# Keys and queries of the second token parity: seven block products in one stage instead of eight in two

## The chip, the core and the metric

The kernel runs on one core of one Trainium2 chip. The metric is the time of one execution on the device in microseconds; the program before has a median of 607.33 us in three runs.

## What is computed

A gated mix of two branches over one sequence of 2048 tokens with 512 channels, all in float32:

```python
g = sigmoid((x * gate_w).sum(-1, keepdims=True))
# A: attention, 32 heads of 16 channels; token s sees the 8 tokens s, s-2, ..., s-14
q, k, v = split(x @ wqkv)                  # 512 -> 3 x 512
logits = einsum(q[s], k[s - 2*w]) * 16**-0.5          # w = 0..7, masked below 0
a = (softmax(logits) @ v) @ wo
# B: gated feed-forward, 1792 hidden channels
b = (gelu(x @ w_gate) * (x @ w_up)) @ w_down
out = g * a + (1 - g) * b
```

## The kernel before

**Order of the work.** Because the window steps by two tokens, even and odd tokens (the two "parities", `par` 0 and 1, 1024 tokens each) never meet, and the kernel does one after the other: `project`/`values` (keys, queries, values, gate), then `ffn(par)` with 14 slices `f` of 128 hidden channels each. Every float32 operand of a product on TensorE is split into a high and a low part ("hi", "lo", both fp32r), and each product is three matmuls: hi x hi, lo x hi, hi x lo. A split is a copy on ScalarE (ACT) for the high part and a subtraction on VectorE (DVE) for the low part; in two places (`operands`, `down_w`) the low part is made with the negated copy on ACT and then a DMA on POOL's queue that adds the raw operand to it.

**Seven products for eight.** The value projection (`values`) and gate/up (`gate_up`) use the Strassen-Winograd scheme: the operands are cut into 2 x 2 blocks, four sums of token blocks (`s1` to `s4`, made by `sums_x`) and four of weight blocks (`t1` to `t4`) are formed, and seven block products take the place of eight. In the second parity the keys and queries are done in the plain way, in two halves of the heads: `project(1)` does the first half, 8 blocks of tokens with `qkv_mm` (4 channel chunks x 3 matmuls each), between the feed-forward part of the first parity and the values; `project_one(1, jj)` does the second half, 8 blocks again, as "pieces" inside the slices f = 0 and 1 of `ffn(1)`. The end of `ffn(0)` up to the beginning of the values of the second parity is called the turn here: the steps `before()`, `again()` and `split_kq()` load and split the tokens and weights of the second parity there.

**Attention.** It is done on DVE alone, head by head group, in 8 units: (0,0) to (0,3) for the first parity, (1,0) to (1,3) for the second. A unit has scores (`scores`, 4 pairs of a product L398 and a reduction L401), a softmax and a weighted sum (`mix`, L436 to L449), and leaves through a scratch tensor `OS` in memory; `channels` reads it back as the operand of the output projection. The generator `attention()` hands its steps out as the matmuls are emitted: every piece of TensorE work ends in `pull(budget)`, and steps are handed out until the budget is used up (a score product counts 2.3). The budgets are written out by hand: `PACE` scales those of `gate_up` and `down`. What is handed out gets a lower priority by `BEHIND` = 150 places, and a scheduler that simulates the program puts the instructions of each engine in their final order. `paced(ins)` tells that scheduler not to put an instruction ahead of the last matmul emitted; it is no wait on the chip.

**The end.** `out_first` does the output projection of the first parity, `down(1, 6, ...)` the last part of the feed-forward product, and `finish` adds the output projection of the second parity, 4 units x 8 token blocks x 3 matmuls (`by_unit`, L868). The last unit's part (1,3) is the last that `finish` needs.

**Buffers that matter here.** 8 banks of PSUM: four named `p`, and `acc0` to `acc3`. `A`, `S`, `d`, `g0`, `g1`, `hh`, `hl`, `c`, `rt` are rings of tiles in SBUF that all stages share.

Of the kernel before, what the change touches and what calls it, by code (L numbers as in the profile page):

```python
# [16 lines left out]
P = 128  # L17
# [12 lines left out]
NU = D // UC  # L30
WARM = 31
BEHIND = 150
PACE = (0.9, 1.12)
LOAD = 4.0
BT = 4
MASKED = -1e9 * DH ** 0.5
# [8 lines left out]
def tile_gated_mix(ctx: ExitStack, tc: tile.TileContext, xt, wqkv, wff, wo, out):  # L45
# [124 lines left out]

    VW, VR, VO, SLOT = 2 * WQ, {}, {}, []

    def room_v():

        for tag, n in ("g0", 3), ("g1", 3), *[("c", 1)] * 4:
# [54 lines left out]
    def fetch_v(n):  # L230
        for i in range(2):
            nc.sync.dma_start(VO[n][i].bitcast(F32), VS_W[n][i])


    z = pool.tile([P, 2, NP], F32, name="z")
# [48 lines left out]
    def values(par, bg, step):  # L284
# [26 lines left out]
        for k, (a, b) in enumerate((("a11", "b11"), ("a12", "b21"), ("s1", "t1"), ("s4", "b22"), ("s2", "t2"),  # L311
                                    ("s3", "t3"), ("a22", "t4"))):
            for t in range(BT):
                if k == 0:
                    C[t] = bank(f"acc{t}")
                elif k == 2:
                    Z_[t] = bank("p")
                ps = Z_[t] if 0 < k < 4 else C[t]
                mm(ps, t, a, b, k in (0, 2))
                if k == 0:  # L320
                    Z_[t] = bank("p")
                    copy(Z_[t][:, :WQ], ps[:, :WQ])
                elif k == 2:
                    PS[t] = stage()
                    copy(PS[t][:, :CU], ps[:, :CU])
                elif k == 3:
                    copy(PS[t][:, CU:], ps[:, :CU])
                elif k == 4:
                    US[t] = stage()
                    copy(US[t][:, CU:], ps[:, :CU])  # L330
                elif k == 5:
                    copy(US[t][:, :CU], ps[:, :CU])
                    nc.vector.tensor_tensor(PS[t], PS[t], US[t], op=OP.add)
                    store(PS[t][:, CU:], t, 1)
                    store(PS[t][:, :CU], BT + t, 1)
                else:
                    if k == 1:
                        ST[t] = stage()
                    jj, st = (t, ST[t][:, :CU]) if k == 1 else (BT + t, ST[t][:, CU:])
                    copy(st, ps[:, :CU])  # L340
                    copy(z[:, par, jj:jj + 1], ps[:, CU:WQ - 1])
                    store(st, jj, 0)
                next(bg, None)
                pull((0.77, 0.63)[par])
            step(k)
        for _ in bg:
            pass
# [3 lines left out]
        nc.vector.tensor_scalar_add(en, en, 1.0)  # L351
        nc.vector.reciprocal(g[:, par], en)
        nc.vector.tensor_scalar(gc[:, par], g[:, par], -1.0, 1.0, op0=OP.mult, op1=OP.add)

    def project_one(par, jj):

# [279 lines left out]
    def down(par, gr, t, b):  # L636
# [20 lines left out]
        elif b:  # L657
            if gr == 0:
                RT[BT + t] = tl("rt")
            nc.scalar.activation(RT[BT + t], pp, AF.Copy)  # L660
        pull(1.2 * PACE[par])

    def gate_up(par, f, pieces, do):

# [48 lines left out]
            hidden((f, 1), ge, c22)  # L713
        late.append(last)

    SPLIT = []

    def again(blk, kc):

        split_x(1, blk, kc, copy=lambda *x: paced(nc.vector.tensor_copy(*x)))  # L720
# [1 line left out]
    def early():  # L722

        t = tl("g0")
        for kc in range(3):
            raw = t[:, kc * 512:(kc + 1) * 512]
            load_kq_weights(raw, kc)
            SPLIT.append((kc, raw))

    def split_kq():  # L730
        kc, raw = SPLIT.pop(0)
        hi, lo = WC[0, kc] = next(room)
        split(nc.vector, hi, lo, raw, held)

    def before():

        room_x(1)
        yield
        again(0, 0)
        yield  # L740
        again(0, 2)
        yield
        split_kq()
        SPLIT.append((3, tl("r")))
        load_kq_weights(SPLIT[-1][1], 3)
        yield
        split_kq()

    def ffn(par):
        XOP.update(((n, kc), X[par, blk, kc + k]) for n, blk, k in (("a11", 0, 0), ("a12", 0, 2), ("a22", 1, 2))  # L750
# [2 lines left out]
        for f in range(FC):  # L753
# [2 lines left out]
            def at(i, x, *args):  # L756
                do.setdefault(i, []).append(lambda: x(*args))

            if f > 1:
# [46 lines left out]
        if par:  # L806
            out_first()
            oT = {}
        for b in range(2):
# [138 lines left out]
    room_v()  # L948
    for _ in sums_x():
        pass  # L950
    made = make_v()
# [32 lines left out]
        store_v()  # L984

    values(0, first(), step)
    room = rooms()
    keep(0)
    ffn(0)
    room_v()  # L990
    for n in "b11", "b21", "t1", "b22", "t2":
        fetch_v(n)
# [53 lines left out]
```

## Time and profile before

| | |
|---|---|
| median of 3 runs (lowest, highest) | 607.33 us (606.11, 609.34) |
| the profiled execution: time, span of its instructions | 604.47 us, 602.7 us |
| TensorE (PE) busy, matmuls | 595.9 us, 2791 |
| VectorE (DVE) busy | 530.4 us |
| ScalarE (ACT) busy | 403.1 us |
| POOL busy | 69.0 us |
| mean granted TensorE clock | 0.999 |
| data moved, mean rate | 132.80 MB, 220 GB/s |

Times in the trace count from the first instruction of the profiled execution. `PEld` is the load of TensorE's stationary operand, which overlaps the matmuls. `x30` behind a row is a count of instructions that were merged into it. The span ends at 602.7 us; the execution's own time is 1.77 us more.

### The profile page before, as it was taken

What the parts mean: (1) busy time and instruction counts of PE and PEld (TensorE: products, weight loads), DVE (VectorE), ACT (ScalarE), POOL (GpSimd) and SP (SyncE); (2) the same over time, 40 slices, a digit from 0 to 9 for tenths busy, and PEclk for the clock granted to TensorE, in tenths of its full rate; (3) what the DMA queues carried; (4) which work ended last, traced back from release to release, by engine and by line L of the source; (5) the groups of instructions that cost most, each with busy time, mean ns of one, the idle gap of its engine ahead of it and who ended that gap; (6) DMA issues with size and microseconds to landing.
All of it is one profiled execution on the core that took longest, in us unless ns stands there. A gap on an engine that the chain in (4) does not pass through costs nothing.

```text
span 602.7 us, 8195 instructions
## 1 busy us (share of the span) xinstructions
PE 595.9 (99%) x2791; PEld 498.3 (83%) x2791; DVE 530.4 (88%) x624; ACT 403.1 (67%) x699; POOL 69.0 (11%) x94
## 2 busy tenths in 40 slices
PE   8999999999999999999999999999999999999997
PEld 6898878888888888888898888888888888888885
DVE  6959899997999979999798989997999799989821
ACT  6665666679777797765574467577666876796531
POOL 0150001111111111102000001111111111101300
PEclk9999999999999999999999999999999999999999
DMA  8695987969686886987599979879596869647813
GB/s 293 237 272 185 310 286 219 248 179 269 182 243 193 242 220 191 264 277 254 179 267 316 305 240 262 213 187 271 149 232 189 260 145 257 167 124 173 139 38 140
DMA packets 85592, 132.80 MB, mean 220 GB/s; under 512 B 8111, under 2 KB 50223, under 8 KB 85550
## 3 DMA queue, kind: packets, MB, share of 16 engines
q1 hardware_dynamic: 66190, 100.88, 50.9%
q0 software_dynamic: 10368, 26.81, 23.6%
q10 hardware_dynamic: 8992, 4.59, 2.6%
q8 instruction: 22, 0.36, 0.2%
q14 instruction: 20, 0.16, 0.1%
HBM read 69.83 MB, written 40.46 MB: 183 GB/s over the span
## 4 chain that ended last, share of the span: by engine, by line
PE 78%; DMA 7%; issue 4%; DVE 4%; ACT 3%; SPq 1%; POOL 1%; ACTq 0%; POOLq 0%
PE p L605 37%; PE acc L647 10%; PE p L647 10%; PE acc L247 9%; PE p L868 5%; PE acc L298 2%; DMA r<-wff 2%; PE acc L868 2%; PE p L247 2%; PE p L298 1%; DVE prod L436 1%; DMA out<-s 1%; DMA raw<-ws 1%; DMA g<-vwt 1%; DMA raw<-xt 1%
## 5 line engine op out<-in xcount | busy, mean ns | idle before, releaser
L605 PE MATMUL p<-S,g 128*128 128x512 f32 x672 | 167.6, 389 | 0.3 <-ACT s L610 0.3
L605 PEld LDWEIGHTS p<-S,g 128*128 128x128 f32 x672 | 125.9, 188 | 26.7 <-ACT s L610 0.7
L605 PE MATMUL p<-A,g 128*128 128x512 f32 x504 | 124.8, 389 | 0.0
L605 PEld LDWEIGHTS p<-A,g 128*128 128x128 f32 x504 | 94.5, 188 | 19.5
L398 DVE TENSOR_TENSOR prod<-kq 128x2048 f32<-128x2048 f32 x32 | 72.9, 2277 | 2.8 <-DMA kq<-kq 2.5
L436 DVE TENSOR_TENSOR prod<-v,lg 128x2048 f32<-128x2048 f32 x32 | 72.9, 2277 | 0.5
L401 DVE TENSOR_REDUCE lg<-prod 128x128 f32<-128x2048 f32 x32 | 73.0, 2281 | 0.2
L647 PE MATMUL p<-d,hh 128*128 128x512 f32 x224 | 69.1, 390 | 0.0
L647 PE MATMUL acc<-d,hh 128*128 128x512 f32 x224 | 59.4, 389 | 0.0
L616 ACT ACTIVATE c<-p 128x512 f32<-128x512 f32 x56 | 33.5, 598 | 38.4 <-PE p L605 38.4
L563 POOL DMA_DIRECT2D g<-raw x28 | 24.2, 863 | 259.1 <-ACT g L560 153.6
L647 PEld LDWEIGHTS p<-d,hh 128*128 128x128 f32 x224 | 42.0, 188 | 9.0 <-ACT p L641 0.3
L647 PEld LDWEIGHTS acc<-d,hh 128*128 128x128 f32 x224 | 42.0, 188 | 8.7
L647 PE MATMUL p<-d,hl 128*128 128x512 f32 x112 | 42.1, 389 | 0.0
L624 DVE TENSOR_TENSOR hl<-c,hh 128x512 fp32r<-128x512 f32 x56 | 38.1, 682 | 3.7 <-ACT hh L623 3.4
L623 ACT ACTIVATE hh<-c 128x512 fp32r<-128x512 f32 x56 | 35.0, 626 | 9.0 <-DVE c L621 7.5
L621 DVE TENSOR_TENSOR c<-c 128x512 f32<-128x512 f32 x56 | 38.2, 683 | 3.1 <-ACT c L712 1.7
L610 ACT ACTIVATE s<-p 128x512 f32<-128x512 f32 x56 | 32.9, 595 | 11.9 <-PE p L605 10.7
L617 DVE TENSOR_TENSOR c<-c,s 128x512 f32<-128x512 f32 x56 | 38.0, 684 | 2.4 <-ACT c L616 2.1
L596 POOL DMA_DIRECT2D d<-r x26 | 22.4, 871 | 152.5 <-ACT d L595 117.3
L440 DVE TENSOR_TENSOR prod<-prod 128x1024 f32<-128x1024 f32 x32 | 39.0, 1218 | 0.2
L660 ACT ACTIVATE rt<-p 128x512 f32<-128x512 f32 x48 | 28.1, 595 | 10.8 <-PE p L647 10.6
(175 smaller groups left out, 965.8 us busy)
## 6 DMA issues: line engine op xcount, KB each, us to landing
g<-raw POOLq DMA_DIRECT2D x28, 512.0 KB, 6.1
raw<-wff SPq DMA_DIRECT2D x42, 256.0 KB, 3.7
ws<-g SPq DMA_DIRECT2D x14, 768.0 KB, 5.4
g<-ws SPq DMA_DIRECT2D x14, 768.0 KB, 6.6
r<-wff SPq DMA_DIRECT2D x28, 256.0 KB, 4.0
d<-r POOLq DMA_DIRECT2D x26, 256.0 KB, 5.2
v<-vs SPq DMA_DIRECT2D x8, 512.0 KB, 6.8
os<-tb SPq DMA_DIRECT2D x64, 64.0 KB, 4.5
```

The source lines that it names most:

```text
L247: LAST[:] = [nc.tensor.matmul(ps[:, :cn], a[:, t], w[:, c0:c0 + cn], start=(kc == 0 and n == 0), stop=(kc == KC - 1 and n == 2))]
L398: paced(nc.vector.tensor_tensor(prod, spans(k, jj), q[:, jj:jj + 2, None, :].to_broadcast([P, 2, W, UC]), op=OP.mult))
L401: nc.vector.tensor_reduce(two_of(lg, jj), prod.rearrange("p j w (h d) -> p (j w) h d", d=DH), axis=AX.X, op=OP.add)
L436: paced(nc.vector.tensor_tensor(prod.rearrange("p j w (h d) -> p (j w) h d", d=DH), spans(v, jj).rearrange("p j w (h d) -> p j w h d", d=D ...
L440: nc.vector.tensor_tensor(prod[:, :, :4], prod[:, :, :4], prod[:, :, 4:], op=OP.add)
L605: LAST[:] = [nc.tensor.matmul(ps, w_, a_, start=(start and kc == 0 and n == 0), stop=(kc == 1 and n == 2), skip_group_check=True)]
L617: nc.vector.tensor_tensor(c, c, s, op=OP.add)
L621: nc.vector.tensor_tensor(ge, ge, up, op=OP.mult)
L623: nc.scalar.activation(hh_, ge, AF.Copy)
L624: nc.vector.tensor_tensor(hl_, ge, hh_.bitcast(F32), op=OP.subtract)
L647: LAST[:] = [nc.tensor.matmul(pp, a[:, ts], w, start=(i == 0 and n == 0 and gr == 0), stop=(i == 1 and n == 2), skip_group_check=True)]
L868: LAST[:] = [nc.tensor.matmul(pa, a, b, start=(first and n == 0), stop=(last and n == 2), skip_group_check=True)]
```

## The change

- `project(1)` and the `project_one(1, jj)` pieces go. A new function `keys` does keys and queries of the second parity, both halves of the heads, by seven block products in one stage between the two parities' other work. The blocks are k = 0 to 6 in the order a11 b11, a12 b21, s2 t2, s3 t3, a22 t4, s1 t1, s4 b22, each with 4 token blocks x 2 chunks x 3 matmuls of 512 columns. After k = 5 and 6, DVE adds a partial result that was copied out before.
- Weights are loaded as blocks (`load_b`); their sums (`combine_b`) and parts are made by `prepare`, one step for each token block of `keys`; `urgent` is its first part. Of the tokens, a21 isn't split any more.
- `split_by_dma` makes a low part by ACT's negated copy and an adding DMA on POOL's queue. It is used for b11, t1, b22, s1 and s4 (two chunks each), and in `load_o` for the four blocks of the output weights, which DVE subtracted before.
- `second` starts the loads for the values after 12 further steps. The values of the second parity no longer carry `last_weights`.
- Stores of the first half's results now go on SP's queue only.
- `down` pulls no attention in the last two of its seven groups in the first parity. `PACE` of the second parity goes from 1.12 to 1.22, the budget of its `values` from 0.63 to 0.75 for each token block; `keys` has 0.2, 0.2, 0.6, 1.0, 1.2, 1.2, 1.2.

```diff
-PACE = (0.9, 1.12)
+PACE = (0.9, 1.22)
...
+    def split_by_dma(hi, lo, raw):
+        paced(nc.scalar.activation(lo, raw, AF.Copy, scale=-1.0))
+        nc.gpsimd.dma_start(lo.bitcast(F32), raw, accum_op=OP.add)
+        held(hi, raw)
...
+    def combine_b(o, x, a, b, kc, op=OP.subtract):
+        paced(nc.vector.tensor_tensor(QR[x, kc], QR[a, kc], QR[b, kc], op=op))
+        QR[o, kc] = QR[x, kc]
...
+    def urgent():
+        room_b("t2")
+        for kc in range(2):
+            for n in "s1", "s3", "s2":
+                sum_x(kc, n)
+            split_s("s2", kc)
+            yield
+            combine_b("t3", "b12", "b22", "b12", kc)
+            combine_b("t2", "b11", "t3", "b11", kc, OP.add)
+            split_b("t2", kc)
+            yield
+        MADE.add("t2")
+        for kc in range(2):
+            split_s("s3", kc)
+            yield
+
+    def prepare():
+        yield from urgent()
+        room_b("t3")
+        for kc in range(2):
+            split_b("t3", kc)
+            yield
+        MADE.add("t3")
+        for kc in range(2):
+            combine_b("t4", "b21", "b21", "t2", kc)
+            combine_b("t1", "b11", "b22", "t2", kc)
+            yield
+        while PHASE[0] < 1:
+            yield
+        room_b("t4")
+        for kc in range(2):
+            split_b("t4", kc)
+            yield
+        MADE.add("t4")
+        while PHASE[0] < 3:
+            yield
+        for kc in range(2):
+            split_s("s1", kc, dma=True)
+            yield
+        room_b("t1")
+        parts_b("t1")
+        MADE.add("t1")
+        yield
+        for kc in range(2):
+            sum_x(kc, "s4")
+            split_s("s4", kc, dma=True)
+            yield
+        room_b("b22")
+        parts_b("b22")
+        MADE.add("b22")
+        yield
...
-                pull((0.77, 0.63)[par])
+                pull((0.77, 0.75)[par])
...
+    def keys(prep, bg):
...
+        for k, (a, b) in enumerate((("a11", "b11"), ("a12", "b21"), ("s2", "t2"), ("s3", "t3"), ("a22", "t4"),
+                                    ("s1", "t1"), ("s4", "b22"))):
+            PHASE[0] = k
+            while k > 1 and b not in MADE:
+                next(prep)
+            if k == 0:
+                C.update((t, bank(f"acc{t}")) for t in range(BT))
+                for t in range(BT):
+                    mm(C[t], t, a, b, 0, True)
+            for t in range(BT):
+                if k == 5:
+                    Z_[t] = bank("p")
+                ps = (Z_ if k in (1, 5, 6) else C)[t]
+                for kc in (1,) if k == 0 else (0, 1):
+                    mm(ps, t, a, b, kc, k == 5)
+                if k == 0:
+                    Z_[t] = bank("p")
+                    nc.scalar.activation(Z_[t], ps, AF.Copy)
+                elif k in (2, 3):
+                    st = (U2 if k == 2 else U3)[t] = tl(next(stages))[:, :512]
+                    nc.scalar.activation(st, ps, AF.Copy)
+                elif k in (5, 6):
+                    st, c = (U3 if k == 5 else U2)[t], tl("rt")
+                    nc.scalar.activation(c, ps, AF.Copy)
+                    nc.vector.tensor_tensor(st, c, st, op=OP.add)
+                    store(st, BT + t if k == 5 else t, 1)
+                else:
+                    st = tl("c" if k == 1 else "rt")[:, :512]
+                    nc.scalar.activation(st, ps, AF.Copy)
+                    store(st, t if k == 1 else BT + t, 0)
+                next(prep, None)
+                if k > 1:
+                    next(bg, None)
+                pull((0.2,0.2,0.6,1.0,1.2,1.2,1.2)[k])
+            if k == 4:
+                done.add((1, 0))
+        for _ in chain(prep, bg):
+            pass
+        done.add((1, 2))
...
-        pull(1.2 * PACE[par])
+        if par or gr < NG - 2:
+            pull(1.2 * PACE[par])
...
+    def tail():
+        again(0, 1)
+        for n in "b12", "b22":
+            for kc in range(2):
+                load_b(n, kc, tl(("hh", "hl")[kc]))
+        yield
+        room_b("b21")
+        split_b("b21", 0)
+        yield
+        again(0, 3)
+        yield
+        split_b("b21", 1)
+        yield
+        for kc in (2, 3):
+            split_x(1, 1, kc, copy=held)
+            yield
...
-                if not par and not b:
-                    split_kq() if t % 2 else again(0, 1 + t)
-                elif not par and b:
-                    again(1, (2, 3, 0, 1)[t])
+                next(ends, None)
...
-            split(nc.vector, hi, lo, raw)
+            split_by_dma(hi, lo, raw)
...
-    project(1, sums_x())
-    for f in range(2):
-        fetch_sums(f)
+    def second():
+        for _ in range(12):
+            yield
+        room_v(1)
+        for n in "b11", "b21", "t1", "b22", "t2":
+            fetch_v(n)
+        yield
+        fetch_d(0)
+        for f in range(2):
+            fetch_sums(f)
+
+    keys(prepare(), second())
...
-    values(1, chain(*(operands(1, 0, i) for i in range(2)), last_weights()), again_v)
+    values(1, chain(*(operands(1, 0, i) for i in range(2))), again_v)
```

More of the change, by code (lines that the diff above doesn't have):

```diff
@@ L232, in fetch_v, with load_b, room_b @@
             nc.sync.dma_start(VO[n][i].bitcast(F32), VS_W[n][i])
+    QR, QO, MADE, PHASE = {}, {}, set(), [0]
+    def load_b(name, kc, raw):
+        QR[name, kc] = raw
+        nc.sync.dma_start(raw, wqkv[int(name[2]) - 1, int(name[1]) - 1, :, kc * 512:kc * 512 + 512])
+    def room_b(name):
+        if name in ("b11", "t2", "t4", "t1"):
+            t = tl("g1", F32R)
+            cols = [t[:, i * 512:(i + 1) * 512] for i in range(4)]
+        else:
+            cols = [*pair("d"), *pair("d")]
+        for kc in range(2):
+            QO[name, kc] = cols[2 * kc:2 * kc + 2]
@@ new lines, in sum_x, with split_s @@
+    def sum_x(kc, n):
+        a11, a12, a21, a22 = (XR[kc][:, i * 512:(i + 1) * 512] for i in range(4))
+        o, a, b, op = {"s1": (a22, a21, a22, OP.add), "s3": (a21, a11, a21, OP.subtract),
+                       "s2": (a11, a22, a11, OP.subtract), "s4": (a12, a12, a11, OP.subtract)}[n]
+        paced(nc.vector.tensor_tensor(o, a, b, op=op))
+    def split_s(n, kc, dma=False):
+        i = {"s1": 3, "s2": 0, "s4": 1, "s3": 2}[n]
+        raw = XR[kc][:, i * 512:(i + 1) * 512]
+        XOP[n, kc] = pair("S")
+        if dma:
+            split_by_dma(*XOP[n, kc], raw)
+        else:
+            split(nc.vector, *XOP[n, kc], raw, held)
@@ L714, in gate_up @@
         late.append(last)
-    SPLIT = []
     def again(blk, kc):
@@ L724, in early @@
         t = tl("g0")
[L725 to L733, printed above, removed]
+        for i, (name, kc) in enumerate((("b11", 0), ("b11", 1), ("b21", 0))):
+            load_b(name, kc, t[:, i * 512:(i + 1) * 512])
     def before():
@@ L808, in ffn @@
             oT = {}
+        ends = iter(()) if par else tail()
         for b in range(2):
@@ L947, in tile_gated_mix @@
     load_v()
-    room_v()
+    room_v(0)
     for _ in sums_x():
```

41 lines of the change are left out of this document (30 added, 11 removed).

## The prediction

> **What bounds the kernel now.** I read the page first, then the chain that ended last, then busy time by stretches, then the order of DVE's and PE's work at the turn and at the end.
>
> ```profile
> span 602.7 us, 8195 instructions
> ...
> PE 595.9 (99%) x2791; PEld 498.3 (83%) x2791; DVE 530.4 (88%) x624; ACT 403.1 (67%) x699; POOL 69.0 (11%) x94
> ```
>
> PE is busy from end to end. Whether it could be packed tighter shows in the chain, whose rows give start, length, and count of matmuls:
>
> ```profile
> 39.20 1.43 PE p L298 x12
> ...
> 327.77 10.88 PE acc L247 x48
> ...
> 395.77 6.80 PE p L605 x30
> ...
> 425.69 6.80 PE p L605 x30
> ```
>
> 6.80/30 and 10.88/48 are both 0.2267 us for a 512-column matmul (1.43/12 = 0.119 for the 258 columns of a value product), and the same place of a slice comes back after (425.69 - 395.77)/2 = 14.96 us, which is 66 matmuls (42 of gate/up, 24 of `down`) at 0.2267. So the slices contain no stall: time goes down only with the number of matmuls, as long as everything else keeps up. DVE is the engine that might not:
>
> ```profile
> 240.00:285.00 45.00, 44.90 (x199) 36.83 (x198) 44.66 (x53) 30.27 (x53) 5.52 (x8) 1.00 0.85 256
> 285.00:303.00 18.00, 18.00 (x84) 15.03 (x83) 14.47 (x27) 10.19 (x18) 1.81 (x4) 1.00 0.55 187
> 303.00:327.00 24.00, 23.80 (x180) 22.57 (x179) 21.84 (x24) 16.10 (x47) 0.88 (x1) 1.00 1.03 315
> 330.00:570.00 240.00, 240.00 (x1060) 198.54 (x1059) 224.19 (x234) 164.75 (x269) 29.95 (x36) 1.00 0.79 208
> 570.00:603.00 33.00, 28.55 (x126) 23.29 (x125) 5.45 (x8) 10.65 (x19) 0.42 (x1) 0.98 0.30 90
> ```
>
> The columns after the length are PE, PEld, DVE, ACT, POOL busy, clock, DMA share, GB/s. DVE is full before the turn (44.66 of 45), has 3.5 us free at it, 15.8 of 240 free in the second parity, and only after 570 is it idle. PE, at a granted clock of 1.00, waits 0.3 us in the first four rows together; so the margins, not the busy share, decide what the change costs.
>
> **Matmuls removed.** The busy time of L247 alone, in the two stretches where the second parity's keys and queries are done:
>
> ```profile
> 277.00:303.50 26.50, 22.54 (x96) 17.87 (x96) 1.00 0.65 215
> 327.00:355.50 28.50, 22.41 (x96) 18.02 (x96) 1.00 0.96 289
> ```
>
> 96 + 96 = 192 matmuls go. `keys` issues 7 blocks x 4 x 2 x 3 = 168 of the same 512 columns with the same kinds of operands (the left 128x128 tile stationary). 24 fewer x 0.2267 = **-5.44 us**. By the Trainium skill, page "TensorE: Matmul & The Clock Gate", section "Back-to-back issue gap", a sustained stream of load and matmul pairs costs about 131 ns at 512 columns; that would be an estimated 3.1 us; this trace doesn't agree, at 226.7 ns, and is used.
>
> **DVE's work.** Rows: a subtraction, the distance between subtractions that follow each other, and a copy to a high part.
>
> ```profile
> 266.08 1.29 DVE L87 TENSOR_TENSOR A<-raw,A 128x512 fp32r<-128x512 f32 x2
> 267.29 0.68 DVE L87 TENSOR_TENSOR g<-g,g 128x512 fp32r<-128x512 f32 x1
> ...
> 278.10 0.75 DVE L720 CAST A<-raw 128x512 fp32r<-128x512 f32 x2
> 278.77 0.68 DVE L624 TENSOR_TENSOR hl<-c,hh 128x512 fp32r<-128x512 f32 x1
> ```
>
> Two follow each other in 1.21 us: 0.605 each; two copies take 0.67: 0.335 each. Before, the second parity's keys and queries and the output weights take 8 copies, 8 token splits, 8 weight splits, 8 sums, 8 splits of sums and 4 output weights: 36 x 0.605 + 8 x 0.335 = 24.5 us. After: 4 copies, 6 token splits, 2 for b21, 8 sums, 4 splits of s2 and s3, 8 weight sums, 6 splits of t2, t3, t4, 8 final additions: 42 x 0.605 + 4 x 0.335 = 26.8 us. DVE gets **2.3 us more** although 14 low parts (b11, t1, b22, s1, s4, output weights) leave it for adding DMAs. It costs PE nothing while the end has margin (below); uncovered, 2.3 us.
>
> **The first sums, at k = 2.** PE gets to k = 2 after 48 matmuls, 10.9 us. `urgent` hands DVE 14 instructions (6 sums, 4 weight sums, 2 + 2 splits), 8.5 us, not before 15 matmuls in the planned order, 3.4 us; so the last low part is there at 11.9, against its first use five matmuls into the product, 12.0. A step of attention in between costs one of these:
>
> ```profile
> 253.34 2.28 DVE L398 TENSOR_TENSOR prod<-kq 128x2048 f32<-128x2048 f32 x1
> ```
>
> This is the first of the eight score steps of unit (0,3), which now lie just ahead of the turn; the budgets of the last two `down` groups, 16 x 1.2 x 0.9 = 17.3, are what the change takes away. With 0.2 for each block at k = 0 and 1 at most one step of 2.28 falls in, and then PE waits 2.2 us. On the other side, the sums are only planned, not made to wait, so an idle DVE runs ahead. Bounds 0 to 2.2 for one step, 4.5 for two; I take 0.7, nearer the lower one since the row 285-303 shows DVE with 3.5 us free even with those steps in.
>
> **The parts by DMA, at k = 5 and 6.** Rows: copies on ACT, the adding DMA on POOL, its landing and that of a plain load.
>
> ```profile
> 297.74 2.70 ACT L86 ACTIVATE S<-raw 128x512 fp32r<-128x512 f32 x5
> ...
> L596 POOL DMA_DIRECT2D d<-r x26 | 22.4, 871 | 152.5 <-ACT d L595 117.3 <-PE p L605 13.7 <-ACT g L86 12.1
> ...
> d<-r POOLq DMA_DIRECT2D x26, 256.0 KB, 5.2
> ...
> r<-wff SPq DMA_DIRECT2D x28, 256.0 KB, 4.0
> ```
>
> Five copies in 2.70 us: 0.54 each in a row. At k = 3 ACT has 4 copies from PSUM, 4 for s1, 4 for t1 and 2 for s4: 14 x 0.54 = 7.6 us in a product of 5.44 us, so it falls 2.1 behind. t1's second negated copy ends 6.7 us after k = 3 began, its DMA lands 5.2 later, at 11.9; PE wants that part at 2 x 5.44 + 1.1 = 12.0. b22 starts from the lag: about 6.0 + 5.2 = 11.2 against 12.0, but if the softmax of unit (0,3) falls into k = 4, its function-table load and an exponential of a copy's length come first:
>
> ```profile
> L416 ACT ACT_TABLE_LOAD x7 | 9.0, 1283 | 0.1
> ```
>
> 1.28 + 0.54 us more: 13.0, a wait of 1.0. Behind those negated copies on ACT stand the copies that empty k = 3's banks, which k = 4 overwrites 4.1 us later; a lag of 2.1 is still covered. On POOL nothing is queued behind but the next such DMA. Bounds 0 to 3 us; I take 0.7. On SP the 32 stores stand ahead of the value weights in emission order, but today those loads are moved up before the end of the feed-forward part, as soon as their tiles are free:
>
> ```profile
> 268.02 1.29 SPq L232 DMA_DIRECT2D g<-vwb  x3
> ```
>
> I take 0, at worst the 2.9 us of one value product (24 x 0.119).
>
> **The end.** The last attention, its way back, and the place where PE needs it:
>
> ```profile
> 569.07 0.71 DVE L449 STREAM_TRANSPOSE tb<-o 128x512 f32<-128x512 f32 x1
> ...
> 574.62 0.34 SPq L846 DMA_DIRECT2D raw<-os  x1
> ...
> raw<-os SPq DMA_DIRECT2D x16, 256.0 KB, 3.1
> ...
> 593.63 0.61 PE L868 MATMUL p<-S,hh 128*128 128x512 f32 x2
> ```
>
> DVE ends attention at 569.8. Its second half is read from 574.6, there at 577.7, and split by 579.1 if ACT is free (a copy and a subtraction, 0.7 us each at most): 9.3 us of way. PE first uses it at 593.6, after the change at 588.2: attention may end as late as 578.9, **9.1 us** later than now. I walked the budgets through the emission order with 0.2267 us a matmul and 0.119 in the values. Today the scores of (0,3) are handed out at 233 and run at 253: DVE drags a queue of some 20 us, so taking 17.3 out of the turn first empties that queue rather than idling DVE. After the change the walk hands out the last step at 557 (today 552), at 10.86 units for a slice against a unit's 41.4, 57 us for each unit. The end comes between 557 (no queue left) and 577 (the old queue of 20): no wait. I take 0.
>
> **Sum.** 602.7 - 5.4 + 0.7 + 0.7 = 598.7 us of span, 600.5 us with the 1.77 around it. The profiled execution was 2.86 us under the median of the runs, so the median goes to 607.33 - 5.44 + 1.4 = **603.3 us**. Without any new stall it is 601.9; a little less is possible, since 0.2 us of PE's waiting for value weights could go too.
>
> **Rivals.**
>
> *Operands late in `keys`* (k = 2, 5, 6 each by 1 to 3 us). For: the three sums above meet their deadlines within 0.1 us, and DMA is full from 303 to 327 (share 1.03). Against: the scheduler may put ready matmuls of the values between, as it does now at the turn. With two attention steps at k = 2 (4.5) and 1.0 for b22 it is 607.33 - 5.44 + 5.5 = 607.4.
>
> *Attention late at the end, slower than before.* If DVE has no queue to empty and the 17.3 taken out of the turn are simply done later, with 2.3 of new work, attention ends at 569.8 + 19.6 = 589.4, 10.5 past 578.9, and `finish` waits: 607.33 - 5.44 + 10.5 = 612.4. It decides from 578.9 on and outweighs the gain from 584.3. For: DVE has just 15.8 us free in 240. Against: the walk above.
>
> *POOL starved by DVE.* The rows show adding DMAs landing in 5.2 us, 1.2 more than plain loads, beside a DVE that is 88% busy. If in the dense stage each of t1 and b22 took 3 us longer, as a queue behind DVE's copies would make it, the sum is 603.3 + 4 = 607.3 (the first 2 us of it meet the margins above). The Trainium skill, page "SBUF — State Buffer", section "SBUF: two separate sides", says that a DMA from GpSimd's queue can't get its descriptors written while DVE holds the shared port, which speaks against moving low parts there. The trace bears it out weakly, at 5.2 against 4.0.
>
> That the change doesn't remove what it says is excluded by the count.
>
> **How the numbers follow.** Forecast (stalls up to 2.4 us, below 604.3) 0.55; operands late 0.22; POOL starved 0.05; attention late 0.16; several of these at once 0.02. A run of this kernel tells about 0.5%, 3.0 us, from no change: faster is the forecast, 0.55; within are the two middle cases, 0.27; slower the last two, 0.18. The forecast's own range is 601.3 to 604.3; upward it must take in late operands and part of late attention, to 611, which leaves out about 0.14 above and 0.04 below.
>
> **What would show it.** PE matmuls 2767; rows of the new stage at 5.44 us a product; DVE busy near 533; the last transpose (now 569.1) at 557 to 577, and no idle of PE at the last unit's products. I am wrong if PE's idle in `keys` is over 2.4 us, with t2, t1 or b22 as releaser, or if PE waits in `finish` for the last `channels`.

## The result, and the profile after

The changed kernel takes 611.45 us (median of 8 runs, 609.59 to 613.77) against 607.07 us (8 runs, 605.89 to 609.34) for the kernel before: a ratio of **1.0072** [1.0044, 1.0101]. Forecast were 603.3 us and a range of 601.0 to 611.0. The time went the other way and ended just outside. The profiled execution took 610.77 us, with a span of 608.0.

The page's first lines after:

```profile
span 608.0 us, 8220 instructions
...
PE 592.7 (97%) x2767; PEld 493.4 (81%) x2767; DVE 534.4 (88%) x626; ACT 419.9 (69%) x734; POOL 80.8 (13%) x108
```

2767 matmuls: the 24 are gone. PE is busy 592.7 of 608.0 us, where it was busy 595.9 of 602.7: idle time rose from 6.8 to 15.3 us. Busy time by stretches, first after, then before (columns as in the prediction: length, PE, PEld, DVE, ACT, POOL busy, clock, DMA share, GB/s), shows where:

```profile
300.00:320.00 20.00, 20.00 (x101) 17.04 (x100) 13.23 (x18) 17.38 (x31) 7.27 (x9) 1.00 1.02 240
320.00:350.00 30.00, 26.86 (x177) 23.83 (x176) 25.00 (x29) 15.51 (x43) 1.35 (x2) 1.00 1.04 304
350.00:380.00 30.00, 27.21 (x121) 21.70 (x120) 25.88 (x27) 21.05 (x36) 3.47 (x4) 1.00 0.99 286
380.00:400.00 20.00, 20.00 (x90) 16.57 (x89) 17.60 (x21) 15.42 (x24) 2.59 (x3) 1.00 0.85 236
```

```profile
300.00:320.00 20.00, 20.00 (x153) 19.28 (x152) 19.76 (x24) 14.44 (x38) 0.88 (x1) 1.00 0.94 269
320.00:350.00 30.00, 29.80 (x143) 24.84 (x142) 27.77 (x26) 13.63 (x28) 0.87 (x1) 1.00 0.96 296
350.00:380.00 30.00, 30.00 (x134) 24.82 (x134) 26.98 (x34) 21.30 (x33) 4.29 (x5) 1.00 0.88 236
380.00:400.00 20.00, 20.00 (x90) 16.57 (x89) 19.80 (x18) 11.76 (x20) 1.72 (x2) 1.00 0.84 222
```

PE idles 3.14 + 2.79 = 5.93 us at 320-380, and 0.20 before. These are the value products and the first slices, behind the new stage. From 300 to 380 the DMA share is 1.02, 1.04 and 0.99, for 0.94, 0.96 and 0.88 before. Bytes alone tell little: at 300-350 the changed kernel moves 13.92 MB for 14.27 before, at 300-390 it moves 25.09 for 23.80. But POOL's queue, which carries the adding DMAs, takes 34.7% of the DMA engines' time at 300-350, for 10.6% before. The chain of the changed kernel, followed back through this stretch, runs mostly over transfers, with some PE work between them that is left out here:

```profile
292.81 14.28 PE acc L474 x63
...
319.15 7.36 DMA ks<-hl
...
326.52 6.11 DMA kq<-ks
...
332.64 5.42 DMA qs<-hl
...
346.43 6.80 DMA g<-ws
...
362.58 10.55 DMA d<-r
```

The first row is the new stage: 63 matmuls in 14.28 us, 0.2267 each, no gap. Then come stores of keys and queries out of the staging tiles `hl`, a load of keys, loads of slice operands and an adding DMA. PE's waits in it (the bracket is the idle time and what ended it):

```profile
322.99 0.97 PE L405 MATMUL p<-c,A 128*128 128x258 f32 x6 [0.75 <-ACT p L412]
335.20 0.99 PE L405 MATMUL p<-g,S 128*128 128x258 f32 x6 [0.76 <-ACT hh L412]
338.61 0.98 PE L405 MATMUL acc<-c,S 128*128 128x258 f32 x6 [1.02 <-ACT hl L412]
347.86 2.19 PE L405 MATMUL acc<-c,A 128*128 128x258 f32 x16 [0.49 <-DMA c<-vwt]
353.37 0.47 PE L772 MATMUL p<-A,g 128*128 128x512 f32 x1 [1.49 <-DMA g<-ws]
...
369.58 1.65 PE L772 MATMUL p<-A,g 128*128 128x512 f32 x6 [1.17 <-DMA g<-raw]
```

The first three name ACT. ACT's own waits say for what it stood still; it copies PSUM into staging tiles whose last contents are still being stored:

```profile
322.06 0.60 ACT L505 ACTIVATE rt<-p 128x512 f32<-128x512 f32 x1 [1.23 <-DMA qs<-rt]
331.64 0.39 ACT L412 ACTIVATE hl<-p 128x256 f32<-128x256 f32 x1 [1.69 <-DMA qs<-hl]
334.77 0.38 ACT L412 ACTIVATE hh<-p 128x256 f32<-128x256 f32 x1 [2.74 <-DMA qs<-hh]
338.17 0.38 ACT L412 ACTIVATE hl<-acc 128x256 f32<-128x256 f32 x1 [2.19 <-DMA qs<-hl]
```

So all six waits come from landings, three of them seen through ACT, which works its copies off in order (the first stands behind the copy at 322.06). The adding DMAs land later too, 6.4 us at the median for 5.2 before:

```profile
d<-r POOLq DMA_DIRECT2D x26, 256.0 KB, 6.4
```

At the end, the last attention step (before: 569.07), its reading back and PE's wait:

```profile
590.99 0.71 DVE L616 STREAM_TRANSPOSE tb<-o 128x512 f32<-128x512 f32 x1
...
595.60 0.35 SPq L1022 DMA_DIRECT2D raw<-os  x1
...
598.63 0.63 ACT L86 ACTIVATE hh<-raw 128x512 fp32r<-128x512 f32 x1 [2.98 <-DMA raw<-os]
...
599.31 1.88 PE L1044 MATMUL p<-S,hh 128*128 128x512 f32 x7 [0.90 <-ACT hh L86]
```

Attention ends 21.9 us later than before, and PE waits for it. Two theories remain: **the crowded stretch** (transfers that nothing covers at 300-390 us) and **late attention** (DVE's chain sets the end). The rivals to the first are SP's queue as such, the adding DMAs as such, and the order within ACT's queue.

In the expectations "lost" time is the sum of what start-to-start distances of neighbouring matmuls exceed 0.2267 us (0.119 for values): 8.3 us at 320-400 after and 0.6 before. It is more than the idle time of the rows above, since ends of matmuls are modelled. A letter for a theory holds within its own text.

### The profile page after: what moved, and what is told of

The parts are those of the page before. It is cut to its first block, busy times and chain, and to the rows that moved or that the text cites. A ratio compares the mean times of both kernels' runs of the same rounds, so it can differ in the third digit from the quotient of the medians.

```text
span 608.0 us, 8220 instructions
## 1 busy us (share of the span) xinstructions
PE 592.7 (97%) x2767; PEld 493.4 (81%) x2767; DVE 534.4 (88%) x626; ACT 419.9 (69%) x734; POOL 80.8 (13%) x108
## 4 chain that ended last, share of the span: by engine, by line
PE 89%; DMA 7%; ACT 2%; issue 1%; DVE 0%; POOL 0%; SPq 0%; ACTq 0%; POOLq 0%
PE p L772 40%; PE p L814 13%; PE acc L814 12%; PE acc L354 5%; PE p L1044 5%; PE acc L474 4%; PE acc L405 3%; PE p L474 2%; PE p L354 2%; DMA d<-r 2%; PE acc L1044 2%; PE p L405 2%; DMA ks<-hl 1%; DMA g<-ws 1%; DMA kq<-ks 1%; DMA qs<-hl 1%
## 5 line engine op out<-in xcount | busy, mean ns | idle before, releaser
L772 PE MATMUL p<-A,g 128*128 128x512 f32 x504 | 126.2, 390 | 3.3 <-DMA g<-ws 1.5
L814 PE MATMUL acc<-d,hl 128*128 128x512 f32 x112 | 35.8, 389 | 0.0
```

The costliest lines, as they stand in the source:

```text
L772: LAST[:] = [nc.tensor.matmul(ps, w_, a_, start=(start and kc == 0 and n == 0), stop=(kc == 1 and n == 2), skip_group_check=True)]
L814: LAST[:] = [nc.tensor.matmul(pp, a[:, ts], w, start=(i == 0 and n == 0 and gr == 0), stop=(i == 1 and n == 2), skip_group_check=True)]
```

## The experiments

All ratios are to the kernel before, run on the same chip. The cuts of code show the main lines of each edit only.

**Attention handed out again** in the last two `down` groups, the rest as changed.

```diff
-        if par or gr < NG - 2:
-            pull(1.2 * PACE[par])
+        pull(1.2 * PACE[par])
```

> The changed kernel, with attention handed out again in the last two groups of down of the first parity (the one condition undone). Theory A (attention ends too late: DVE idled about 11 us between 270 and 320 while unit (0,3) was unfinished, and the last step ended at 591.7, where 569.8 was the place before): the last transpose comes 8 to 17 us earlier, PE's wait of 1.1 us in finish goes, and the time falls by 2 to 4 us to 607 to 609; it can't fall further since the 9 us of stalls of PE from 320 to 375 stay. Theory B (the stalls of PE from 320 to 375 alone set the time): the time stays within 1 us of 611.4. Rival C (the turn needs DVE free): PE idles between 280 and 322, where it has no gap now, and the time rises above 613.

1.0172 [1.0111, 1.0233]. Busy time by stretches:

```profile
280.00:290.00 10.00, 10.00 (x46) 8.28 (x45) 9.70 (x15) 7.99 (x15) 3.48 (x7) 1.00 0.50 206
290.00:300.00 10.00, 5.65 (x19) 4.20 (x18) 9.40 (x18) 7.42 (x13) 0.00 (x0) 0.79 0.66 191
```

PE stands still for 4.35 us at the third product, the size the prediction gave for two steps of attention there (4.5). Keeping attention out of the turn is needed for `keys`. The loss at 320-400 stays (7.7 us).

Attention does not end earlier, though theory A expected 8 to 17 us: it ends at 594.4 (591.7 in the changed kernel). Unit (0,3) ends at 331.2, as in the kernel before (330.9), but then DVE stands still, with only the sums of the values between:

```profile
330.51 0.71 DVE L616 STREAM_TRANSPOSE tb<-o 128x512 f32<-128x512 f32 x1
...
347.10 0.69 DVE L440 TENSOR_TENSOR hl<-hl 128x512 f32<-128x512 f32 x1 [13.50 <-ACT hl L412]
...
358.19 2.29 DVE L565 TENSOR_TENSOR prod<-kq 128x2048 f32<-128x2048 f32 x1 [8.60 <-PE p L772]
...
593.69 0.71 DVE L616 STREAM_TRANSPOSE tb<-o 128x512 f32<-128x512 f32 x1
```

The third row is the first score product of unit (1,0). It names PE, but its last operand, the queries, landed at 358.07; in the changed kernel they landed at 337.30 and in the kernel before at 320.66. So the withheld steps alone don't make attention late: the second parity's keys and queries also come later.

**Only that part, in the kernel before**: the same condition around its `pull`.

> The kernel before, with only one part of the change: no attention is handed out in the last two groups of down of the first parity. Theory A: DVE idles about 10 us around the turn, attention ends about 17 us later than 569.8, at 583 to 588, where PE can take it only up to about 584: the time rises by 0 to 4 us, to 607 to 611, with a wait in finish. Theory B: attention isn't a limit, the time stays within 1 us of 607.1.

1.0003 [0.9981, 1.0026]. The last transpose, 569.07 before:

```profile
585.50 0.71 DVE L449 STREAM_TRANSPOSE tb<-o 128x512 f32<-128x512 f32 x1
```

16.4 us later, for 17.3 taken out: nearly all of it comes back. It does not come back at the turn: unit (0,3) ends 2.9 us later, unit (1,2) 16.3 later, and DVE is idle for 10.1 of the 50 us at 450-500 (4.5 before). So DVE had room; it looks as if the place of the steps in the planned order makes the delay, which no run here isolates. It costs nothing there only because PE needs it late: its way back took 7.2 us (9.3 in the prediction), to 593.4, and PE doesn't wait.

**A lighter end**: of the last unit's four score steps two are left out.

```diff
-        for jj in range(0, NP, 2):
+        for jj in range(0, NP // 2 if light else NP, 2):
```

> The changed kernel, with half of the scores of unit (1,3), two products and two reductions, left out (they are set to zero): about 8.8 us less for DVE near the end. Theory A in part: PE's wait of 1.1 us in finish and the late last stores go, the time falls by 1 to 3 us to 608.5 to 610.5, and what is left over the forecast's 603 is PE's stalls from 320 to 380. If attention alone set the time it would fall by 5 us or more; if it had no part, by less than 0.5.

1.0050 [1.0027, 1.0073]. The last transpose is at 584.62, PE doesn't wait at the end, but the idle time at 320-380 stays (7.8 us in this execution, 5.9 in the changed kernel). Late attention alone is worth some 0.2% while the crowded stretch stands, which the two intervals don't tell from nothing.

**Other queues.** Stores of the first half of the heads (k = 1 and 4) on ACT's queue:

```diff
-            nc.sync.dma_start(rows(KS[1, hh][:, W:], jj), two[:, 0])
+            queue = nc.sync if hh else nc.scalar
+            queue.dma_start(rows(KS[1, hh][:, W:], jj), two[:, 0])
```

> The changed kernel, with the 16 stores of the first half's keys and queries (k = 1 and 4) on ACT's queue, as before the change, and not on SP's. Theory B1 (SP's queue is the jam: it issues without a pause from 305 to 360, and the stores of k = 5 and 6 leave late, so their staging tiles are free late and ACT can't empty the banks of the value products): PE's lost time from 320 to 350 falls from 4.6 us to under 2. Theory B2 (the DMA engines are the jam, share 1.05 from 310 to 380): it stays over 3.5 us, as the bytes are the same. For the time, theory A expects no more than 1.5 us either way, since attention ends at the same place; theory B alone expects as much less as PE's stalls shrink, 3 us or more.

1.0134 [1.0066, 1.0203]: a loss of 6.0 us appears at 260-320, and 6.9 stays at 320-400. ACT was blocked instead (PE stood still for 5.31 us behind it), so this says little of SP. Next, loads of the value weights and of the first two slices' sums on POOL's queue:

```diff
-        nc.sync.dma_start(VO[n][i].bitcast(F32), VS_W[n][i])
+        nc.gpsimd.dma_start(VO[n][i].bitcast(F32), VS_W[n][i])
```

> The changed kernel, with the loads of the second parity's value weights and of the first two slices' sums issued from POOL's queue and not from SP's. The bytes are the same. Theory B1 (SP's queue is the jam): the stores leave earlier, PE's lost time from 320 to 380, 8.3 us, falls below 5. Theory B2 (the 16 DMA engines are full, share 1.0 to 1.1 from 310 to 380): it stays at 7 to 10 us, or grows as POOL's DMAs wait for each other in order.

1.0065 [1.0043, 1.0087]: no different. One large stall, at the low part of `s4`, whose adding DMA took 11.2 us, took the place of several (1.89 us of idle time are left at 350-380):

```profile
326.77 3.78 PE L474 MATMUL p<-d,S 128*128 128x512 f32 x8 [5.39 <-DMA S<-raw]
```

So SP's queue as such is not the cause.

**Low parts back on DVE**: all 14 subtracted by DVE.

```diff
-            split_by_dma(*QO[name, kc], QR[name, kc])
+            split(nc.vector, *QO[name, kc], QR[name, kc], held)
```

> The changed kernel, with all low parts that it makes by adding DMAs (b11, t1, b22, s1, s4, output weights: 14) subtracted on DVE again. DVE gets 8.5 us more, of which 2.4 at the end, ACT loses 14 copies, the DMA queues lose 14 x 256 KB. Theory B2 (DMA engines jammed): PE's lost time from 320 to 375 falls by 1 us or more. Theory A: the last transpose comes up to 6 us later and the time rises by 1 to 6 us. If neither sees a change over 1 us, the adding DMAs are of no account here.

1.0166 [1.0082, 1.0251]. The loss at 320-400 falls by 2.0 us, the one at the end rises to 5.3, since attention ends at 595.6: the time is only moved.

**Less DMA work, in two ways and together.** Five of the seven value weights not loaded; then the adding DMAs of `keys` left out (`NOADD` is set while `keys` is emitted; eight lie in it, the expectation counts ten); then both.

```diff
-        for n in "b11", "b21", "t1", "b22", "t2":
+        for n in "b11", "b21":
             fetch_v(n)
+        VO.update((n, VO["b11"]) for n in ("t1", "b22", "t2", "t3", "t4"))
```

> The changed kernel, but only two of the seven value weight operands of the second parity are loaded (4 DMAs for 14), and the other five products use the first one's: 10 x 258 KB less to move, 2.6 MB, about 9 us at the 288 GB/s of that stretch, and 10 issues less on SP. Theory B2: PE's lost time from 320 to 380 falls from 8.3 us to under 4. Theory A (attention, which ended at 591.7, holds the end): the time falls by no more than 3 us from 611.4, since PE then waits in finish for the last unit. If A is wrong the time falls by as much as PE's stalls, 4 us or more.

1.0114 [1.0072, 1.0156]. The stalls at 350-400 go, but ACT now meets an operand copy (L727) that waits 5.49 us for a load, with the copies of the value products behind it.

```diff
-        nc.gpsimd.dma_start(lo.bitcast(F32), raw, accum_op=OP.add)
+        if not NOADD[0]:
+            nc.gpsimd.dma_start(lo.bitcast(F32), raw, accum_op=OP.add)
```

> The changed kernel, but in the keys' stage the ten adding DMAs (s1, t1, s4, b22 and the rest of that stage) are left out: the low parts there are only the negated copies, so this part of the computation is wrong and only the time is read. ScalarE's copies and VectorE's work stay as they are. Theory D (the bytes and slots of the adding DMAs fill the DMA engines at 300-320 us, and the stores and loads behind them come late): the PE time lost at 320-400, 8.3 us in the changed kernel, falls to 3 or less, and the time to 605.5-607.5. Theory Q (in-order queues: ScalarE's copies stand behind one that waits for a staging tile or a load, whatever the adding DMAs do): the loss stays at 6.5 or more and the time at 609.5-611.5. Theory B (it is the 21.8 us of load-free products that are gone as cover): a fall of the loss by about the DMA time that is gone, 10 x 256 KB at some 300 GB/s over an 80 us full stretch, 1-3 us: 608.5-610.5.

1.0101 [1.0042, 1.016]. The stalls moved again, most of them to the adding DMAs of the `down` weights:

```profile
363.21 0.50 PE L818 MATMUL acc<-d,hh 128*128 128x512 f32 x1 [1.70 <-DMA d<-r]
...
383.93 0.50 PE L818 MATMUL acc<-d,hh 128*128 128x512 f32 x1 [1.76 <-DMA d<-r]
```

Each alone bought nothing. Both:

> The changed kernel with two parts left out at once: the ten adding DMAs of the keys' stage (low parts there are only negated copies) and five of the seven loads of value weights (those products reuse the first's operands). Its output is therefore not the reference's; only the time is read. Theory B (the DMA work of 300-390 us as a whole bounds the stretch; each part alone only moved the stall to the next landing): the loss at 320-400 falls from 8.3 to 3 or less, the granted clock is back at 0.999, the time 605-607.5 with the wait at the end left. Theory Q (order in the queues, not the amount): the loss stays at 5 or more and the time at 610-613.

1.0009 [0.9986, 1.0031], busy time by stretches:

```profile
320.00:350.00 30.00, 29.90 (x202) 27.55 (x201) 27.87 (x31) 18.92 (x50) 1.76 (x2) 1.00 0.89 250
350.00:380.00 30.00, 30.00 (x134) 24.85 (x133) 27.56 (x30) 22.23 (x37) 4.30 (x5) 1.00 0.93 271
380.00:400.00 20.00, 18.79 (x83) 15.22 (x82) 18.84 (x22) 12.69 (x20) 1.72 (x2) 1.00 0.76 187
```

1.31 us of idle time left, at a DMA share of 0.89 for 1.04 at 320-350. So the DMA work as a whole makes the stalls: with one part gone PE waited for transfers that neither cut touches, and with both gone these come in time too, but for the 1.31 us. Which transfer PE waits for changes with every edit. Attention still ends at 590.7.

**Both causes removed.** First the value weights and the lighter end:

> The two reliefs of the runs before together: two of the seven value weights loaded, and half the scores of unit (1,3) left out. If the two causes cover each other (each hides the other's relief), the time falls by more than the sum of the two single falls, to 602 to 605, where the forecast without stalls lies (602 to 603). If they simply add, it falls by the sum.

1.0052 [1.0031, 1.0073]: as with the lighter end alone. Then all three cuts:

> The run without the ten adding DMAs and with two of seven value weights, and in addition half the scores of the last unit (1,3) left out, so that attention is not late at the end; the output is not the reference's, only the time is read. If the DMA work of 300-390 us and attention's delay are the whole miss: TensorE does not wait in the finish, the loss behind 260 us is 2.5 or less, and the time is 603-605, the forecast before the experiments being 603.3. If something else took part of it: 606 or more.

**0.9944** [0.9924, 0.9963]: 602.32 us against 605.66. Applied to 607.07 it is 603.7 us (602.5 to 604.8), and the forecast was 603.3. The last transpose is at 580.07, PE doesn't wait for the last unit, and idles 1.77 us at 320-400. One new wait of 2.18 us stands at 552.18 in the profiled execution (605.51 us, the slowest of seven), behind the exponential on ACT, so the loss is over the 2.5 us expected. Less work is done in this kernel than in the one before, so this bounds what a mended version could reach; it is no such version.

**The cover put back**: 96 matmuls that nobody reads, where `project_one` stood.

```diff
-                pieces = [()] * 4
+                pieces = [[lambda jj=jj: spare(jj) for jj in jjs]
+                          for jjs in (((0, 1), (2, 3), (4, 5), (6,)), ((7,), (), (), ()))[f]]
```

> The changed kernel, with 96 extra matmuls in the first two slices of the second parity's feed-forward stage, where project_one stood before the change; they read an operand that is there already and nobody reads their sums. They cost 96 x 0.2267 = 21.8 us of TensorE, and attention is handed out beside them as project_one did (2.2 us per twelve). Theory B (project_one's products covered loads, staging and attention's delay): the loss at 350-400 (3.7 us) and the wait at the end (1.2 us plus 1.6 us of longer tail) are mostly gone, so the time rises by 15.5-18.5 us, not 21.8: 627-630. Theory Q or D (queues or adding DMAs, no matter what covers them): the rise is 20.5-22: 632-633.5.

1.0383 [1.0342, 1.0423]: 18.9 us more than the changed kernel's ratio gives ((1.0383 - 1.0072) x 607.07), not 21.8, and above the 15.5 to 18.5 expected. The two intervals leave 16 to 22 us, so the time alone doesn't show that 2.9 us of it hid something. The profile points that way: the wait for the last unit is gone (one of 1.37 us for a copy on ACT stands at 570.19), 350-380 idles 1.51 us for 2.79. The value products stand ahead of the cover and idle as in the changed kernel (3.77 us at 320-350). Cover is at most a part of the cause; cover ahead of the value products was not tried.

**Attempts at a better version.** The adds from PSUM (no copy into `rt`); s4 and s1 made earlier; larger budgets at k = 3 to 6; s1 and s4 on DVE with these budgets; eight high parts on DVE; these with the loads on POOL's queue.

```diff
-                    nc.vector.tensor_tensor(st, c, st, op=OP.add)
+                    nc.vector.tensor_tensor(st, ps, st, op=OP.add)
```

> The changed kernel, but at the sixth and seventh products of the keys VectorE adds straight from PSUM: eight ScalarE copies into the tag rt are gone, and with them the waits of ScalarE for the landing of the stores out of rt (1.46 and 1.23 us at 315 and 322 us). Theory Q (in-order queues): the 0.91 us stall of TensorE at 321.85 goes and part of the ones behind it at 334-337; lost time at 320-350 from 4.6 to 2.5-3.5, time 609.3-610.8. Theories B and D (DMA is full, who waits is a side issue): the same wait turns up behind the next staging tile; lost time at 320-350 within 0.7 of 4.6, time 611-612.

1.0216 [1.0169, 1.0264], the worst: without waits at `rt` ACT reached the ring `hl` sooner and waited 6.3 us for one store, which took 8.5.

```diff
-        while PHASE[0] < 3:
-            yield
         for kc in range(2):
+            sum_x(kc, "s4")
+            split_s("s4", kc, dma=True)
```

> The changed kernel, but the low parts of s4 and s1 (four adding DMAs, eight ScalarE copies) are made as soon as t4 is, with the third product instead of the fourth and fifth: where the DMA engines are busy 0.50-0.68 and not 0.94-1.10. Theory D (adding DMAs in a full stretch): the loss at 320-400 falls from 8.3 to 4-6, the raw tiles come free earlier, the loads of the sums start up to 10 us earlier, time 607.5-609.5. Theory Q (queues, not place of the adds): loss within 1 of 8.3, time 610.5-612. Against both: the copies may delay the third product's own operands, then a stall shows at 290-300.

1.0150 [1.0095, 1.0206]: now the parts of t1 came late, and PE waited in `keys`:

```profile
317.82 4.38 PE L474 MATMUL p<-g,S 128*128 128x512 f32 x11 [2.35 <-DMA g<-g]
```

```diff
-                pull((0.2,0.2,0.6,1.0,1.2,1.2,1.2)[k])
+                pull((0.2,0.2,0.6,1.2,1.6,1.6,1.6)[k])
```

> The changed kernel with larger budgets of attention in the keys' fourth to seventh product (1.2, 1.6, 1.6, 1.6 for 1.0, 1.2, 1.2, 1.2), where VectorE idled 6.8 us in 300-320. If attention's delay at the end is worth what the run with a lighter end showed: the last transpose moves from 591.0 to 585-588, the wait in the finish (1.2 us) and half of the longer tail go, time 608.5-610.5. If the stretch before the values is bound by VectorE's operands (as with the pulls handed back, 617.5): a stall at 300-325 of 1-4 us and 611.5-615.

1.0108 [1.0066, 1.0151]: the last transpose came no earlier (594.1, in an execution that was already 2.8 us later at its first transpose). What idles DVE most in `keys` isn't the budget but the exponential, which in the changed kernel stands on ACT behind copies:

```profile
313.05 0.69 DVE L584 TENSOR_REDUCE m<-lg 128x64 f32<-128x512 f32 x1 [5.49 <-ACT lg L583]
```

```diff
-            split_s("s1", kc, dma=True)
+            split_s("s1", kc)
```

> The last kernel's budgets, and s1 and s4 subtracted by VectorE (four subtractions of 0.6 us, 2.4 us of VectorE; four adding DMAs fewer, the tiles of raw sums free earlier). If the adding DMAs' own landings delay the loads into the raw tiles: the loads of the slices' sums start some 5 us earlier, loss at 320-400 from 8.3 to 5-6.5, time 607-609.5. If the amount of DMA work in the stretch is what counts: four of some 60 transfers, loss 7-8.5, time 609.5-611.5.

1.0193 [1.0128, 1.0257]: that wait fell to 1.25 us, attention still ended late (596.4), and 7.6 us were lost at 350-400.

```diff
-        held(hi, raw)
+        if PHASE[0] >= 3:
+            paced(nc.vector.tensor_copy(hi, raw))
```

> The changed kernel, but the eight high parts of s1, t1, s4 and b22 are copied by VectorE (0.335 us each, 2.7 us, where it idles 5.49 us waiting for the exponential) and not by ScalarE (0.54 each, 4.3 us). If ScalarE's backlog is what delays the exponential: the wait before the reduction behind it falls from 5.49 to 2.5 or less, the last transpose comes 1-3 us earlier (588-590), the wait at the end shrinks, time 609-611. If attention's end is set by the budgets alone: last transpose 591-593.5, time 611.5-613.

1.0168 [1.0147, 1.0188]: the wait for the exponential fell to 2.89, near the 2.5 expected, and more than that came back at the next ring (1.46 us in the changed kernel):

```profile
322.22 1.17 ACT L508 ACTIVATE rt<-p 128x512 f32<-128x512 f32 x2 [7.51 <-DMA qs<-rt]
```

> The last kernel, and the value weights and the sums of the first two slices loaded on POOL's queue. If both reliefs add up: last transpose 587-589.5, no wait at the end, time 607.5-609.5, near the kernel before. If the DMA work of 300-390 us as a whole is what bounds it: a stall of 4-6 us at 320-330 as in the run with those loads alone, time 610-612.

1.0148 [1.0109, 1.0187], with 10.82 us of the same wait. No version beat the kernel before. In the three runs that relieved ACT (adds from PSUM, high parts on DVE, these with POOL's loads) it stood still longer for a store out of one of its rings: 6.3, 7.5 and 10.8 us.

## Why the prediction was wrong

- **Matmuls removed, -5.44 us:** right. 2767 matmuls, the new stage at 0.2267 us each without a gap; with both causes removed the time is 603.7.
- **DVE's work, +2.3 us:** right in sign; busy time rose by 4.0 (530.4 to 534.4).
- **First sums and parts by DMA, 0.7 + 0.7 us:** too dear. `keys` has no stall, so the rivals "operands late" and "POOL starved" didn't happen either. ("Operands late" says that all three deadlines were met within 0.1 us; by the sums above it, b22's margin was 0.8.) The danger at k = 2 was real, as the run with attention handed out again shows.
- **"On SP ... I take 0, at worst the 2.9 us": the step that failed first.** It looked at when the value weights may start, and not at how much must land between 300 and 390 us. Before, only half of the 32 key and query stores came ahead of the value products; the other 16 were issued at 339 to 356, beside `project_one`, whose 21.8 us of matmuls need nothing loaded. After the change these 16 are issued at 319 to 340, beside the value products, eight more adding DMAs stand ahead of them, and `project_one` is gone. The 192 matmuls were counted as work removed; that 96 of them could cover transfers was not, though the run with the cover put back shows only a part of this. It cost 5.7 us of idle time in the profile. Taking DMA work out alone moves the ratio by 0.0063 (1.0072 to 1.0009), 3.8 us.
- **"Empties that queue rather than idling DVE": the second step that failed.** DVE did idle, 16.6 us from 240 to the end of unit (0,3) (6.0 before), and that unit ended 16.3 us later. Attention ended at 591.7, not 557 to 577. The kernel before with this edit alone shows a delay of 16.4 for 17.3. But giving the steps back to the changed kernel did not bring the end forward: the keys and queries of unit (1,0) land 16.6 us later than before (337.30 for 320.66), a term that the walk of the budgets doesn't have. How the 21.9 us split between the two stays open.
- **The rival "attention late"** had named the place and almost the moment (589.4), from the withheld steps and DVE's 2.3 us, without the later keys and queries, so that its nearness is in part luck. Its price, 10.5 us, took PE to be on time at 588.2. PE came late itself, because of the stalls, so the wait shrank to 0.9 us.
- **The two overlap.** Attention ended at 590 to 592 with and without the stalls (591.7 and 590.7), which alone puts the span at about 606 (606.3 without most of the stalls). So removing one shows the other: -0.2% for late attention with the stalls there (within the noise), -0.65% (1.0009 to 0.9944) once they are gone. Together it is 0.0128 x 607.07 = 7.8 us, against a miss of 611.45 - 603.3 = 8.2.

What stays open, beside that split: which order of transfers would fit the stretch, and how much DMA work has to go. DMA was busy only 0.50 and 0.68 at 280-300 in the changed kernel, but nothing I moved there helped. Larger rings for `rt`, `hh` and `hl` were not tried.

## What to carry to other kernels

Matmuls that need no fresh data are cover for the transfers beside them: before removing or moving them, list what lands in that stretch and what hides it then. Work withheld from a nearly full engine can come back almost whole at the end of its chain (16.4 us for 17.3 here), so compare that end with the first use, on both sides of the change; and ask when the inputs of its next piece of work land, since giving the work back is no help where they are later. Where one cut moves a stall to another transfer and leaves the time, cut two things at once before giving up the theory that the transfers as a whole bound it.

## What was not expected of the hardware

A stall of PE costs more than itself. In the run with the adds from PSUM, the stretches before, in and behind a stall (the clock is the third column from the end):

```profile
330.00:334.80 4.80, 4.80 (x37) 4.58 (x36) 4.59 (x5) 1.15 (x3) 0.00 (x0) 1.00 1.01 361
334.80:339.40 4.60, 0.41 (x2) 0.00 (x0) 2.34 (x2) 0.25 (x1) 0.00 (x0) 0.83 0.95 309
339.40:343.40 4.00, 3.82 (x10) 3.10 (x11) 0.00 (x0) 3.05 (x8) 0.86 (x1) 0.50 1.00 228
343.40:350.00 6.60, 6.60 (x41) 6.05 (x40) 4.66 (x8) 4.18 (x8) 0.00 (x0) 0.91 1.08 284
```

Behind a stall of 4.4 us the granted clock is 0.50 for some 4 us, and 10 matmuls (four of 258 columns and six of 512, 1.84 us at the usual pace) take 3.82. The row of the run with early sums shows the same behind 2.35 us: 11 matmuls in 4.38 us, 0.40 each. The Trainium skill, page "TensorE: Matmul & The Clock Gate", section "What's actually happening", says that the clock goes to half after an idle window of about 3.4 us and comes back after one of work. The halving agrees with these rows; the length of the stall doesn't tell when it comes. The run with larger budgets, behind a stall of 1.88 us, and the run with the lighter end, behind one of 2.82 us:

```profile
356.00:360.00 4.00, 3.91 (x13) 3.44 (x14) 2.79 (x3) 2.07 (x4) 0.00 (x0) 0.57 1.04 356
```

```profile
371.00:375.00 4.00, 3.66 (x16) 3.05 (x17) 1.24 (x3) 1.00 (x2) 0.00 (x0) 1.00 1.07 357
```

What else decides is not shown here. Behind the changed kernel's own stalls at 320-380, up to 1.49 us, the clock stayed at 1.00. Its executions with a mean clock of 0.998 or 0.999 took 609.6 to 612.1 us, those with 0.992 to 0.997 took 610.8 to 613.8.

An adding DMA of 256 KB, 5.2 us at the median before, took 11.2 in the crowded stretch (with the loads on POOL's queue), and a store of 128 KB took 8.5 (with the adds from PSUM).
